# Zero stores at other spots: three behind the first group's loads, one behind the last dwd store, four ahead of the last group's first dv store

## The chip, the cores and the metric

The kernel runs on one core of one Trainium2 chip. The metric is device time of one execution in microseconds (us), lower is better.

## The reference, cut to what matters

The reference is the forward and the backward pass of one decode layer: attention of four tokens over a window of 1024 of 4096 cached keys and values, plus a gated feed-forward block, with gradients of all inputs.

```python
W = min(4096, max(256, Sk // 4))                 # 1024 of 4096
k = jnp.repeat(k_cache[:, :, Sk - W:, :], rep, axis=1)
v = jnp.repeat(v_cache[:, :, Sk - W:, :], rep, axis=1)
...
return x + _A_ref(xn, A_k_cache, A_v_cache, A_wq, A_wo) + _B_ref(xn, B_w_gate, B_w_up, B_w_down)
```

The gradients of the two caches have the caches' full shape, (4, 8, 4096, 128) in bf16. Three quarters of each are zeros, because the window does not reach them. These zeros need no arithmetic, but they are 48 MiB that must be written. They go out from one zeroed tile as 32 stores of 1.5 MB, and the kernel is free to place these stores anywhere in the order of its transfers.

## The kernel before

One queue (SyncE) issues nearly all loads and all large stores, in program order. `zero(n)` puts the next n zero stores into it:

```python
def zero(n=1):
    for _ in range(min(n, len(zlist))):
        og, b, g = zlist.popleft()
        store(nc.sync, og[b, g:g + ZR, 0:K0, :].rearrange("g (m j) d -> m g (j d)", m=P // ZR), ztile[:], "zeros")

nc.gpsimd.memset(ztile[:], 0.0)
zero(2)                                  # behind the loads of weights and of group 0
...
def piece_d(f4, i, n, held):             # one of the four stores of dwd (out_8)
    ...
    if i == 3:
        store(nc.sync, out_8[...], held["osb"]..., "rest")
        zero(f4 == 1)
...
for t in range(NT):                      # four groups
    kv_steps(t, 0, 0)
    ...
    softmax(t)
    kv_steps(t, 1, 1)
    if t == NT - 1:
        zero(3)                          # ahead of the last group's dv stores
    link(len(chain))
    ...
tick(len(bg))
zero(len(zlist))                         # what is left
```

Each dv and dk store (1 MB, staged in one of three buffers) is followed by one more zero store. The names in the profile: `ztile` is the zeroed tile, `osb_d`, `osb_g`, `osb_o`, `osb_q` are the output buffers of the weight gradients (four in rotation), `stg_dv` and `stg_dk` those of the cache gradients.

## Time and profile before

| | before |
|---|---|
| time, median of the first 3 runs | 284.95 us (284.8 to 285.53) |
| span of the profiled run | 283.4 us |
| TensorE, VectorE, ScalarE busy | 71%, 58%, 42% |
| moved by DMA | 112.12 MB, mean 396 GB/s |
| last compute instruction begins | 247.7 us |

A large transfer runs on all 16 DMA engines of the core, and the trace has one landing per engine for it. I quote the *median landing* (the ordinary engine), the *last landing* (the slowest), and the *lag*, the difference of the two. The landings carry no engine's name: "the slow engine" is the one that lands last.

### The profile page before, as it was taken

To read this page: it belongs to the slowest core of one execution; us is meant where nothing else is said; L and a number is where in the kernel's file an instruction comes from. 1 tells how busy PE (TensorE), PEld (TensorE's weight loads), DVE (VectorE), ACT (ScalarE), POOL (GpSimd) and SP (SyncE) were. 2 spreads that over 40 slices of the span, in tenths; PEclk is the share of its full clock that TensorE was granted. 3 is DMA by queue.
4 is the path that set the end of the run, shared out by engine and by line. 5 is a ranking of instruction groups with operands and counts; after the bars stand their busy time and mean duration, and the time that the engine had idled before them with its cause. 6 is when DMAs were issued, how large, how long until landed. Compare 5 with 4: busy or idle time off the path is not lost.

```text
span 283.4 us, 6866 instructions
## 1 busy us (share of the span) xinstructions
PE 200.5 (71%) x2972; PEld 137.3 (48%) x2972; DVE 163.4 (58%) x313; ACT 117.8 (42%) x219; POOL 40.1 (14%) x40
## 2 busy tenths in 40 slices
PE   0275799998798899998993799889995997300000
PEld 0264576765466754676752467665564743100000
DVE  7946646676857455767561576766776288900000
ACT  2021476662156077635371464438661387200000
POOL 8600000043011700020700002130004000000000
PEclk9999579999999999999999599999999799955555
DMA  7999989999999999999999999999999989999993
GB/s 266 391 376 433 432 334 369 370 418 351 366 428 409 419 422 422 426 427 417 410 387 423 423 426 430 410 425 404 397 415 377 415 337 420 426 418 415 422 418 153
DMA packets 19565, 112.12 MB, mean 396 GB/s; under 512 B 1664, under 2 KB 4496, under 8 KB 11088
## 3 DMA queue, kind: packets, MB, share of 16 engines
q1 hardware_dynamic: 17744, 103.56, 89.5%
q0 software_dynamic: 1632, 6.29, 5.6%
q10 hardware_dynamic: 160, 1.84, 1.8%
q8 instruction: 23, 0.38, 0.5%
q14 instruction: 6, 0.05, 0.0%
HBM read 30.68 MB, written 81.01 MB: 394 GB/s over the span
## 4 chain that ended last, share of the span: by engine, by line
PE 30%; issue 19%; DMA 18%; DVE 12%; POOL 5%; ACT 3%; DVEq 0%; POOLq 0%; ACTq 0%
DMA out_dram<-stg_dv 11%; DMA wq_sb<-in_A_wq_dram 7%; PE kv_ps L484 6%; PE T_ps L279 5%; PE od_ps L450 4%; PE S_ps L345 4%; DVE dS_s L367 2%; DVE T_sb L98 2%; PE dwq_ps L520 2%; POOL ztile L167 2%; DVE wqT L98 2%; PE pT_ps L279 2%; PE acc_ps L256 1%; PE dwo_ps L505 1%; DVE P_s L367 1%
## 5 line engine op out<-in xcount | busy, mean ns | idle before, releaser
L98 DVE COPY T_sb<-T_ps 128x1024 bf16<-128x1024 bf16 x64 | 44.1, 688 | 24.9 <-PE T_ps L279 24.7
L97 ACT CAST stg_dk<-kv_ps 128x512 bf16<-128x512 f32 x52 | 29.1, 588 | 26.3 <-PE kv_ps L484 11.5
L97 ACT CAST stg_dv<-kv_ps 128x512 bf16<-128x512 f32 x51 | 28.1, 588 | 25.1 <-PE kv_ps L484 24.4
L484 PE MATMUL kv_ps<-qmr,dS_s 128*128 128x512 bf16 x64 | 23.0, 396 | 7.3 <-ACT stg_dk L97 6.6
L463 POOL TENSOR_TENSOR o_s<-od_r,msk_r 128x512 bf16<-128x512 bf16 x8 | 9.1, 1158 | 107.9 <-DVE od_r L455 78.6
L484 PE MATMUL kv_ps<-domr,P_s 128*128 128x512 bf16 x64 | 21.1, 379 | 0.0
L279 PE MATMUL T_ps<-ident,vb 128*128 128x128 bf16 x256 | 20.3, 225 | 0.3 <-DVE T_sb L98 0.3
L279 PEld LDWEIGHTS <-vb 128*128 128x128 bf16 x256 | 17.2, 101 | 4.9 <-issue 2.7
L279 PE MATMUL T_ps<-ident,kb 128*128 128x128 bf16 x256 | 19.5, 219 | 0.0
L279 PEld LDWEIGHTS <-kb 128*128 128x128 bf16 x256 | 16.7, 98 | 4.2 <-issue 0.9
L97 ACT CAST osb_q<-dwq_ps 128x512 bf16<-128x512 f32 x25 | 14.5, 586 | 8.3 <-PE dwq_ps L520 7.4
L329 POOL TENSOR_TENSOR domr<-r,msk 128x1024 bf16<-128x1024 bf16 x4 | 7.6, 1892 | 68.4 <-DVE r L326 62.0
L97 ACT CAST osb_o<-dwo_ps 128x512 bf16<-128x512 f32 x24 | 13.8, 586 | 4.4 <-PE dwo_ps L505 3.6
L97 ACT CAST osb_g<-dwg_ps 128x512 bf16<-128x512 f32 (+1 forms) x25 | 12.5, 541 | 6.6 <-PE dwg_ps L673 5.0
L98 DVE COPY wgT<-wgT_ps 128x1024 bf16<-128x1024 bf16 x14 | 9.6, 686 | 7.7 <-PE wgT_ps L279 7.7
L345 PE MATMUL S_ps<-T_sb,qm 128*32 128x256 bf16 x128 | 12.7, 386 | 0.6 <-DVE T_sb L98 0.5
L345 PE MATMUL S_ps<-T_sb,dom 128*32 128x256 bf16 x128 | 12.7, 387 | 0.1
L98 DVE COPY woT<-woT_ps 128x1024 bf16<-128x1024 bf16 x16 | 11.0, 686 | 2.6 <-PE woT_ps L279 2.2
L98 DVE CAST stg_dk<-kv_ps 128x512 bf16<-128x512 f32 x12 | 7.9, 686 | 7.8 <-DMA out_dram<-stg_dv 7.2
L505 PE MATMUL dwo_ps<-dyr,o_s 128*128 128x512 bf16 x32 | 11.9, 388 | 0.5 <-DVE stg_dk L98 0.2
L520 PE MATMUL dwq_ps<-od_r,xnm 128*128 128x256 bf16 x64 | 11.6, 274 | 0.2 <-ACT osb_q L97 0.2
L98 DVE COPY wqT<-wqT_ps 128x1024 bf16<-128x1024 bf16 x16 | 10.5, 685 | 1.8 <-PE wqT_ps L279 1.6
(188 smaller groups left out, 377.7 us busy)
## 6 DMA issues: line engine op xcount, KB each, us to landing
out_dram<-ztile SPq DMA_DIRECT2D x32, 1536.0 KB, 19.4
kb<-in_A_k_cache_dram SPq DMA_DIRECT2D x8, 1024.0 KB, 15.7
vb<-in_A_v_cache_dram SPq DMA_DIRECT2D x8, 1024.0 KB, 20.7
out_dram<-stg_dv SPq DMA_DIRECT2D x8, 1024.0 KB, 16.7
out_dram<-stg_dk SPq DMA_DIRECT2D x8, 1024.0 KB, 16.1
out_dram<-osb_o SPq DMA_DIRECT2D x8, 512.0 KB, 19.0
out_dram<-osb_q SPq DMA_DIRECT2D x8, 512.0 KB, 11.6
out_dram<-osb_g SPq DMA_DIRECT2D x8, 448.0 KB, 7.9
```

The costliest lines, as they stand in the source:

```text
L97: return nc.scalar.copy(out=out, in_=in_)
L98: return nc.vector.tensor_copy(out=out, in_=in_)
L167: nc.gpsimd.memset(ztile[:], 0.0)
L279: nc.tensor.transpose(ps[:, i, :], a, ident[:])
L329: nc.gpsimd.tensor_tensor(out=mr[:].rearrange("p g q d -> p (g q) d"), in0=r4[:, k, :].unsqueeze(1).broadcast_to([P, SL, Dh]), in1=msk[:]. ...
L345: nc.tensor.matmul(ps[b * RB:(b + 1) * RB, :], lhsT=zt[:, b * GP + g, c0:c0 + RB], rhs=T_sb[:].rearrange("p (x b) -> p b x", b=B)[:, b, :] ...
L367: nc.vector.scalar_tensor_tensor(out=out[:], in0=src[:].unsqueeze(2).broadcast_to([P, WQ, B]), scalar=rr[:, 0:1], in1=mskb[:].unsqueeze(1) ...
L450: nc.tensor.matmul(od_ps[g * 32:g * 32 + B * rep, k, g, :], lhsT=cols[:, jj, g * NQ + q, :], rhs=blks[(t, g)][:, j, :], start=(j == 0), st ...
L463: nc.gpsimd.tensor_tensor(out=o_s[:, g], in0=rows[:, g].unsqueeze(1).broadcast_to([P, rep, Dh]), in1=msk_r[:].unsqueeze(2).broadcast_to([P ...
L484: nc.tensor.matmul(mps[:].rearrange("p q d -> p (q d)"), lhsT=src[:, j * P:(j + 1) * P], rhs=mr[:, g].rearrange("p q d -> p (q d)"), start ...
L505: nc.tensor.matmul(mps[:], lhsT=o_s[:, g].rearrange("p r d -> p (r d)")[:, i:rep * Dh:rep], rhs=dyr[:], start=True, stop=True)
L520: nc.tensor.matmul(mps[:, i].rearrange("p g d -> p (g d)"), lhsT=xnm[:, i2 * 2 + i, c * P:(c + 1) * P], rhs=dq_r[:].rearrange("p g d -> p ...
```

## The change

Its intent is to have zero stores queued where the queue waits for compute and the DMA engines run out of work. The number of zero stores stays 32; three come forward from the end.

```diff
     nc.gpsimd.memset(ztile[:], 0.0)
-    zero(2)
+    zero(3)
...
-            zero(f4 == 1)
+            zero(f4 % 2)
...
             if t == NT - 1:
-                zero(3)
+                zero(4)
```

Below, these three lines are called the front part, the dwd part and the late part.

## The prediction

> **What bounds the kernel now.** I read the page first, for the share of each engine and of the transfers, then the stretches of a microsecond each, for where the transfers pause, then the order of issue on the store queue, and last the landings of single transfers. No engine is near full on the page (TensorE 71%, VectorE 58%, ScalarE 42%). The row of the 16 DMA engines is:
>
> ```profile
> DMA  7999989999999999999999999999999989999993
> DMA packets 19565, 112.12 MB, mean 396 GB/s; under 512 B 1664, under 2 KB 4496, under 8 KB 11088
> ```
>
> Transfers are busy in nearly every slice, and compute stops near 248 us of 283 us: the chain of waits itself ends there, with the last small VectorE work, and behind it only stores run. So the bytes set the end, and time is won only where a DMA engine has nothing to do. The store queue in order of time (start us, length us, then what is issued):
>
> ```profile
> 18.55 1.69 SPq L103 DMA_DIRECT2D out_dram<-ztile  x2
> 37.73 3.53 SPq L103 DMA_DIRECT2D out_dram<-osb_d  x2
> 41.31 0.55 SPq L103 DMA_DIRECT2D out_dram<-ztile  x1
> ...
> 43.08 3.79 SPq L103 DMA_DIRECT2D out_dram<-osb_d  x2
> 49.16 0.33 SPq L103 DMA_DIRECT2D out_dram<-osb_g  x1
> ...
> 214.72 3.80 SPq L103 DMA_DIRECT2D out_dram<-ztile  x3
> 228.66 0.54 SPq L103 DMA_DIRECT2D out_dram<-stg_dv  x1
> ...
> 253.96 6.89 SPq L103 DMA_DIRECT2D out_dram<-ztile  x5
> ```
>
> The queue issues in program order and blocks on the first store whose data is not there. It stands still before 37.73, 49.16 and 228.66, and five zero stores are left for the end. In stretches of 1 us (the last two columns are the mean busy share of the 16 DMA engines and GB/s) the transfers issued before run out just there:
>
> ```profile
> 40.00:41.00 1.00, 1.00 (x19) 0.86 (x18) 0.60 (x2) 0.98 (x3) 0.00 (x0) 1.00 0.39 156
> 41.00:42.00 1.00, 1.00 (x21) 0.77 (x18) 0.60 (x2) 0.98 (x3) 0.00 (x0) 1.00 0.38 152
> 46.00:47.00 1.00, 1.00 (x20) 0.76 (x18) 0.69 (x1) 0.81 (x3) 0.00 (x0) 1.00 0.82 340
> 49.00:50.00 1.00, 0.85 (x14) 0.61 (x14) 0.69 (x2) 0.40 (x1) 0.00 (x0) 1.00 0.25 72
> 228.00:229.00 1.00, 0.97 (x13) 0.47 (x10) 0.75 (x3) 1.00 (x3) 0.00 (x0) 1.00 0.27 111
> 229.00:230.00 1.00, 0.97 (x28) 0.86 (x29) 0.69 (x2) 0.13 (x1) 0.00 (x0) 1.00 0.43 176
> 278.00:279.00 1.00, 0.00 (x0) 0.00 (x0) 0.00 (x0) 0.00 (x0) 0.00 (x0) 0.50 0.53 221
> 279.00:280.00 1.00, 0.00 (x0) 0.00 (x0) 0.00 (x0) 0.00 (x0) 0.00 (x0) 0.50 0.09 37
> 280.00:281.00 1.00, 0.00 (x0) 0.00 (x0) 0.00 (x0) 0.00 (x0) 0.00 (x0) 0.50 0.09 37
> 281.00:282.00 1.00, 0.00 (x0) 0.00 (x0) 0.00 (x0) 0.00 (x0) 0.00 (x0) 0.50 0.03 12
> ```
>
> The reader is to see two things. There are three holes, at 40 to 42, at 49 and at 228 to 230, and the change puts a zero store ahead of each. And the end is not even: from 279 us the share is 0.09, which is one or two engines of 16, for another 3 us. A single slow DMA engine ends the program.
>
> The trace has sixteen landings for each transfer, which measures that engine. I give the median landing and how far behind it the last one is. Last zero store: median 279.06, last 282.29, 3.2 us behind, second-last only 0.9 us behind. The third of the zero stores issued from 214.72: median 228.75, last 234.15, 5.4 us behind. The dv store after it: median 232.83, last 236.65. Median to median that is 4.1 us for a 1 MB store; last to last it is 2.50 us. The later 1 MB stores, with no hole in front, took 2.5 us from the last landing of the transfer ahead to their own (240.45 to 243.03, 246.74 to 249.23). So the slow engine worked straight through the hole at 228, and the other fifteen waited.
>
> **What the Trainium skill says.** "DMA: Bandwidth & Descriptors", section "Why a DMA increments its semaphore by 16 and not by 1", says that a DMA runs on up to 16 engines "that finish independently", and only the full count means landed; the spread of 0.3 to 6 us between landings agrees. The same page, "Where 436 GB/s comes from", puts the ceiling at 435 GB/s; the steady stretches here (423 to 436 GB/s, 260:270 at 436) are at it, so filling holes is the only gain from moving stores. "Issuing engines are not separate DMA queues" says that all issuers share the same 16 engines; here the weight loads that GpSimd issues took 15.4 and 21.8 us to land among the stores, which agrees.
>
> **The change part by part.** No store is added or removed: 32 zero stores of 1.5 MB each before and after. Comparing the order of instructions, nothing moves on TensorE, VectorE, ScalarE and GpSimd but buffer numbers; only the store queue differs. One zero store takes about 3.7 us of all engines (median landings of the last three: 271.64, 275.37, 279.06). The five at the end become two.
>
> Third zero store behind the loads: it is queued at about 20 to 22 us, so the engines have 3.7 us more to do when they would run dry at 40. The hole is (1-0.39)+(1-0.38) = 1.23 us on the mean engine, and it is filled. What is over (2.5 us) also carries across the dips at 46 (0.18) and 49 (0.75).
>
> The zero store behind the last dwd store: its 3.7 us lie where the first has already closed the hole. I give it nothing of its own; it makes the queue longer between 50 and 70.
>
> Fourth zero store ahead of the last dv stores: the hole at 228 to 230 is 0.73+0.57 = 1.30 us on the mean engine and is filled.
>
> Sum on the mean engine: 1.23+0.18+0.75+1.30 = 3.46 us. That would be the gain if all engines ended level.
>
> On the engine that ends last it is less. The 1.30 us at 228 count nothing, because that engine had no pause there. From about 126 us its landings follow one another without a gap that the transfers do not explain. What counts is its pause before 56 us. At 40 us the last engine is 2.2 us behind the median, more than the hole, so it lost next to nothing; the ordinary engines lost 1.2 to 1.6 us there and up to 0.9 us at 46 to 49. By 56 us the spread is down to 0.35 us: the laggards had caught up while the others waited. I cannot tell from the landings whether the engine last at the end is one of the two behind at 40 (gain about 0.4 us, for part of the second hole) or an ordinary one (about 1.2+0.9 = 2.1 us). With fourteen of sixteen ordinary, but the same engine perhaps slow throughout, I take 1.5 us. The stated prediction is 284.95-1.5 = 283.4 us.
>
> **Costs.** Stores of dwd and dwg/dwu land later: two more zero stores are 7.4 us of transfers, less about 2 us of holes, so some 5.4 us by 60 us. The output buffers come free that much later. Before, ScalarE waited 1.3 us for one of them near 64 us; after, some 3 to 5 us there, and the load of the next group's weights is issued later with it. This moves compute, not the end: queue and compute move by the same amount, and compute has room at the end, as the slow engine has 12.9 us of landings (249.84 to 262.8) between the issue and the landing of the first of the last dwq stores. The fourth zero store makes the last dv store land up to 2.4 us later (3.7 less the 1.3 of the hole), and the last dk evictions wait for its buffer; the two zero stores left at the end cover it.
>
> **Rivals.** (1) All engines gain alike, and 3.46 us go: 281.5 us. For it speaks the mean share; against it the last landings. (2) The slow engine has no pause at all and its work is fixed: no gain, 284.5 to 285 us. For it speaks the 2.2 us lag at 40; against it that the last engine may change. (3) The later buffers stall TensorE long enough that its clock falls (it reads 0.51 at 155 to 160 us after a pause) and a store comes late with the queue dry: a new hole of 1 to 3 us, 285 to 287 us. Against it: the queue is longer everywhere. (4) With the queue deeper, the small dips at 196, 205 and 216 close as well, about 1.2 us on the mean engine: 280.3 us. Against it: compute is held by landings (the dv store issued at 132.9 landed at 156.5 and held ScalarE 6.7 us), so it shifts with the queue.
>
> **Range and chances.** Between rival 1 and a little above rival 2: 281.9 to 285.1 us. Faster by over 2% needs under 279.3 us, more than all the holes named: 0.03. Slower by over 2% needs 290.7 us: 0.02. Within 2%: 0.95.
>
> **What would show it.** Shares of 0.9 and more at the first hole and at the last (which comes about 5 us later); a gap between median and last landing of the final zero store that is larger than 3.2 us, 5 us or so, with a longer tail of 0.06 to 0.09 behind the bulk; more wait of ScalarE for output buffers near 64 us; compute ending 5 to 8 us later. Wrong would be: a last gap that stays at 3 us with the end 3 us earlier (rival 1), or a share under 0.5 in a new place (rival 3).

## The result, and the profile after

| | before | after |
|---|---|---|
| time, median of 4 runs each | 285.12 us | 283.03 us (282.93 to 283.69) |
| span of the profiled run | 283.4 us | 281.0 us |
| last zero store: median landing | 279.06 us | 274.50 us |
| last zero store: last landing | 282.29 us | 279.94 us |
| lag | 3.2 us | 5.5 us |

The ratio is 0.9931 (95% interval 0.991 to 0.9951), so the change is worth about 2.0 us. Ratios here are the mean time of one kernel's fast runs over that of the other's of the same rounds, so they are not quite the ratio of the medians quoted.

The two landings tell the story in one row each. The ordinary DMA engine is done 4.56 us earlier. The slowest engine is done 2.35 us earlier, and that is what the time followed.

The landings also tell where the slowest engine won this. Each zero store put ahead of a transfer should delay it by some 3.7 us; what is missing of that delay is gain. The first dwg store (`osb_g`, two more zero stores ahead of it) landed last at 57.90 us instead of 52.36, so 7.4-5.54 = 1.9 us were won by then. The dwq store that landed last at 222.33 us before came at 227.32: 7.4-4.99 = 2.4 us (in between, the figure wavers from 1.7 to 4.4). The last dwq store, with three more ahead, came at 272.69 instead of 264.01: 11.1-8.68 = 2.4 us. So the slowest engine won nothing from the late hole. For the median landing, the same two dwq stores give 2.4 and 4.6 us.

The row of DMA slices of the kernel after, to be set against that of before. The 8s of slices 6 and 33 are gone, and the last slice is a 0, where for most of it only one engine still works:

```profile
DMA  7999999999999999999999999999999999999990
```

The store queue of the kernel after. The third zero store follows the first two, one comes at 46.42, four at 219.74, and two are left at the end:

```profile
18.53 3.75 SPq L103 DMA_DIRECT2D out_dram<-ztile  x3
38.12 2.64 SPq L103 DMA_DIRECT2D out_dram<-osb_d  x2
...
46.42 0.71 SPq L103 DMA_DIRECT2D out_dram<-ztile  x1
48.67 0.34 SPq L103 DMA_DIRECT2D out_dram<-osb_g  x1
...
219.74 4.40 SPq L103 DMA_DIRECT2D out_dram<-ztile  x4
233.63 0.54 SPq L103 DMA_DIRECT2D out_dram<-stg_dv  x1
...
263.25 1.98 SPq L103 DMA_DIRECT2D out_dram<-ztile  x2
```

The same in stretches of 1 us (the last three columns: TensorE's granted clock, mean busy share of the 16 DMA engines, GB/s):

```profile
40.00:41.00 1.00, 1.00 (x20) 0.76 (x18) 0.69 (x1) 0.98 (x3) 0.00 (x0) 1.00 1.04 434
49.00:50.00 1.00, 1.00 (x24) 0.82 (x20) 0.27 (x2) 0.89 (x2) 0.00 (x0) 1.00 0.95 393
201.00:202.00 1.00, 1.00 (x12) 0.52 (x12) 0.78 (x2) 0.75 (x2) 0.00 (x0) 1.00 0.47 193
210.00:211.00 1.00, 1.00 (x14) 0.64 (x10) 0.36 (x2) 0.86 (x4) 0.00 (x0) 1.00 0.40 160
233.00:234.00 1.00, 0.94 (x13) 0.45 (x10) 0.75 (x2) 1.00 (x3) 0.00 (x0) 1.00 0.93 393
274.00:275.00 1.00, 0.00 (x0) 0.00 (x0) 0.00 (x0) 0.00 (x0) 0.00 (x0) 0.50 0.24 98
275.00:276.00 1.00, 0.00 (x0) 0.00 (x0) 0.00 (x0) 0.00 (x0) 0.00 (x0) 0.50 0.06 25
278.00:279.00 1.00, 0.00 (x0) 0.00 (x0) 0.00 (x0) 0.00 (x0) 0.00 (x0) 0.50 0.06 25
```

The hole at 40 went from a share of 0.39 to 1.04, the one at 49 from 0.25 to 0.95. The late hole, which would now lie some 5 us later than 228, is closed (0.93). The mean engine has deeper dips than before at 201 and 210. They cost the slowest engine nothing: between 200 and 222 us (times of before) the gain of the last landing, reckoned as above, stays at 2.4 us, while that of the median falls from 4.5 to 2.4. From 275 to 279 the share is 0.06, which is one engine of sixteen at 25 GB/s, alone.

What the change cost: the gradients' output buffers come free later. Waits between 40 and 90 us for a store to land before its buffer could be written, in the kernel after (who waits, for what, us in total, times, longest):

```profile
ACT osb_g L97 <- DMA out_dram<-osb_g: 3.2, 1, 3.2
DVE osb_g L98 <- DMA out_dram<-osb_g: 2.9, 1, 2.9
ACT osb_g L97 <- DMA out_dram<-osb_d: 2.0, 1, 2.0
```

Before, there was one such wait of 1.3 us. Compute ends later (the last instruction begins at 257.21 instead of 247.74; about half of that comes from the late part, as is shown below), and the end does not care.

### The profile page after: what moved, and what is told of

Its sections match the earlier page's. It is cut to its first block, busy times and chain, and to the rows that moved or that the text cites. A ratio compares the mean times of both kernels' runs of the same rounds, so it can differ in the third digit from the quotient of the medians.

```text
span 281.0 us, 6867 instructions
## 1 busy us (share of the span) xinstructions
PE 203.1 (72%) x2972; PEld 138.8 (49%) x2972; DVE 164.1 (58%) x313; ACT 117.8 (42%) x219; POOL 40.1 (14%) x40
## 4 chain that ended last, share of the span: by engine, by line
PE 47%; DMA 22%; DVE 16%; ACT 4%; issue 2%; SPq 0%; DVEq 0%; ACTq 0%
DMA out_dram<-stg_dv 13%; PE T_ps L279 8%; PE kv_ps L484 7%; DMA wd_sb<-in_B_w_down_dram 6%; PE S_ps L345 5%; PE od_ps L450 5%; DMA out_dram<-osb_g 4%; DVE T_sb L98 3%; DVE dS_s L367 2%; PE wdT_ps L279 2%; PE dwq_ps L520 2%; PE acc_ps L256 2%; PE dwd_ps L660 2%; DVE P_s L367 2%; PE wgT_ps L279 2%
## 5 line engine op out<-in xcount | busy, mean ns | idle before, releaser
L484 PE MATMUL kv_ps<-qmr,dS_s 128*128 128x512 bf16 x64 | 23.9, 414 | 11.3 <-ACT stg_dk L97 10.6
L279 PE MATMUL T_ps<-ident,kb 128*128 128x128 bf16 x256 | 20.4, 225 | 0.0
L279 PEld LDWEIGHTS <-kb 128*128 128x128 bf16 x256 | 17.5, 101 | 4.5 <-issue 1.3
L484 PEld LDWEIGHTS <-dS_s 128*128 128x128 bf16 x64 | 6.2, 101 | 12.2 <-issue 11.1
```

The source lines that it names most:

```text
L279: nc.tensor.transpose(ps[:, i, :], a, ident[:])
L484: nc.tensor.matmul(mps[:].rearrange("p q d -> p (q d)"), lhsT=src[:, j * P:(j + 1) * P], rhs=mr[:, g].rearrange("p q d -> p (q d)"), start ...
```

## The experiments

Two theories. **A**: the one DMA engine that lands last sets the end, and a hole costs time only where that engine, too, has nothing to do. **B**: the end follows the mean engine, and each hole that is filled is worth its missing share.

### The front part alone

```diff
-    zero(2)
+    zero(3)
```

> Only the third zero store behind the first group's loads; the others stay as before. Theory A (the DMA engine that lands last sets the end, and only its pauses before 56 us count): the holes at 40 to 42 and at 49 us close, and most of the whole gain of 2.1 us comes from here, 1.5 to 2.1 us, about 283.2 us; the last landing of the last zero store comes 1.5 to 2.1 us earlier. Theory B (all engines gain what the mean engine's holes are worth): 1.23+0.18+0.75 = 2.16 us of gain here too, but with the median landing and the last one moving alike; the two theories differ in the last lag, about 4 to 5 us under A and 3.2 us under B.

Measured: 283.73 us against 285.5 us of before in the same rounds, ratio 0.9927 (0.9909 to 0.9944), 2.1 us. Last zero store: median 274.48, last 280.91, lag 6.4 us. So this line alone brings the whole gain. The median moved 4.6 us and the last landing 1.4 us in the profiled run, so they do not move alike; that is against B. The lag is above what A expected (4 to 5 us), and the 1.4 us are a little under its 1.5 to 2.1; the profiled run was the slowest of the six (283.97 us).

### The dwd part alone

```diff
-            zero(f4 == 1)
+            zero(f4 % 2)
```

> Only the zero store behind the last dwd store. It is issued near 46.4 us, after the hole at 40 to 42 us, so it can close the dip at 46 and the hole at 49 us alone. Theory A: 0.3 to 0.9 us of gain, about 284.5 us. Theory B: 0.93 us, about 284.2 us. If the first-hole pause is what the slow engine lost, this run keeps nearly all of the time of before.

Measured: 285.23 us against 285.5 us, ratio 0.9981 (0.9967 to 0.9996), 0.5 us by the ratio. Last zero store: median 278.38, last 281.92. The first hole stays open (share 0.31 at 40 us), the one at 49 is closed. Half a microsecond is in A's range; B's 0.93 us is near the edge of the interval. This run alone does not decide between them.

### The late part alone

```diff
             if t == NT - 1:
-                zero(3)
+                zero(4)
```

> Only the fourth zero store ahead of the last group's first dv store. Theory A: no gain, within 0.3 us of before (285.1 us), although the hole at 228 to 230 us closes; the median landing of the last zero store comes about 1.3 us earlier, the last landing stays, the lag grows from 3.2 to about 4.5 us. Theory B: 1.3 us of gain, 283.8 us, lag unchanged at 3.2 us.

Measured: 285.95 us against 285.5 us, ratio 1.001 (0.9997 to 1.0023). No gain. The stretches of this run at the place of the hole and at its end:

```profile
228.00:229.00 1.00, 0.94 (x13) 0.45 (x11) 0.78 (x2) 1.00 (x3) 0.00 (x0) 1.00 1.02 430
229.00:230.00 1.00, 1.00 (x28) 0.83 (x29) 0.68 (x2) 0.06 (x1) 0.00 (x0) 1.00 0.91 381
...
276.00:277.00 1.00, 0.00 (x0) 0.00 (x0) 0.00 (x0) 0.00 (x0) 0.00 (x0) 0.50 0.58 246
277.00:278.00 1.00, 0.00 (x0) 0.00 (x0) 0.00 (x0) 0.00 (x0) 0.00 (x0) 0.50 0.14 61
...
281.00:282.00 1.00, 0.00 (x0) 0.00 (x0) 0.00 (x0) 0.00 (x0) 0.00 (x0) 0.50 0.06 25
```

The hole at 228 to 230 is gone, the bulk of the stores ends two microseconds earlier (median landing 277.06 instead of 279.06), and the last landing is at 282.89 instead of 282.29. The lag is 5.8 us (A had expected 1.3 us for the bulk and a lag of 4.5). A gain of the ordinary engines, here 2.0 us, was worth nothing. This refutes B, whose 1.3 us lie far outside the interval.

### The front and the dwd part without the late part

```diff
-    zero(2)
+    zero(3)
...
-            zero(f4 == 1)
+            zero(f4 % 2)
```

> The first two parts together, without the late one. Theory A: the whole gain, 2.0 us, 283.0 us, equal to the changed kernel within 0.3 us. Theory B: 2.16 us, 1.3 us slower than the whole change is under B, so 284.3 us when scaled to the measured whole of 2.1 us.

Measured: 283.67 us against 285.5 us, ratio 0.993 (0.9911 to 0.9949), the whole gain. The late hole is open again (shares of 0.50, 0.21 and 0.55 from 232 to 235 us). Last zero store: median 276.41, last 279.82. The ordinary engines end 1.9 us later than in the kernel after, the slowest 0.1 us earlier.

### Making the late hole larger on purpose

If A holds, a much larger hole at the same place must still be free as long as the slow engine bridges it. The kernel after was taken, with two zero stores there, and then with one:

```diff
-                zero(4)
+                zero(2)        # second kernel: zero(1)
```

> The changed kernel with two zero stores instead of four ahead of the last group's first dv store; two more stand at the end. The other fifteen DMA engines then run dry about 5 us before that dv store: without the fourth store the hole was 1.3 us, and one store less adds 3.7 us. Theory A (the engine that lands last sets the end): it is about 6.0 us behind there in the changed kernel, so it still bridges the hole and the time stays within 0.5 us of the changed kernel (283 us), with the lag cut from 5.5 to 0.5 to 1.5 us at the end. Theory B (mean engine): 5 us lost, about 288 us.

> The same with one zero store there. Hole of the ordinary engines 1.3+2x3.7 = 8.7 us. Theory A: only what exceeds the lag of 6.0 us is lost, some 2 to 3.5 us, about 285.5 to 286.5 us, and the lag at the end falls under 1.5 us. Theory B: 8.7 us lost, about 291.7 us.

> The changed kernel again, for the same chip and rounds as the two above. Both theories: ratio to before near 0.993, 283 to 283.7 us.

Measured in the same rounds, before at 285.93 us:

| zero stores ahead of the last group's first dv store | time | ratio to before | last zero store: median / last landing |
|---|---|---|---|
| four (the changed kernel again) | 283.16 us | 0.9906 (0.9886 to 0.9926) | 274.76 / 279.96 |
| two | 283.90 us | 0.9931 (0.9907 to 0.9954) | 279.29 / 280.19 |
| one | 288.24 us | 1.0086 (1.0063 to 1.0108) | 284.36 / 285.22 |

With two stores, the hole of that run:

```profile
229.00:230.00 1.00, 1.00 (x15) 0.75 (x12) 0.73 (x2) 0.52 (x1) 0.00 (x0) 1.00 0.37 148
230.00:231.00 1.00, 0.99 (x12) 0.58 (x9) 1.00 (x2) 0.65 (x3) 0.00 (x0) 1.00 0.15 53
231.00:232.00 1.00, 1.00 (x15) 0.70 (x12) 0.85 (x2) 1.00 (x4) 0.00 (x0) 1.00 0.06 25
232.00:233.00 1.00, 0.94 (x13) 0.45 (x11) 0.81 (x2) 1.00 (x3) 0.00 (x0) 1.00 0.06 25
```

For two microseconds fifteen engines stand still and one works at 25 GB/s. On the mean engine 3.4 us are missing in these four lines. The ordinary engines end 4.5 us later than in the changed kernel, the time is 0.7 us worse (a little over A's 0.5, far from B's 5). The lag at the end fell to 0.9 us: the hole spent nearly all of it. The packets show that the slow engine did not pause: its last packet of the zero stores ran to 234.81 us, and its first packet of the dv store began there.

With one store, the slow engine runs dry as well:

```profile
228.00:229.00 1.00, 0.78 (x6) 0.29 (x4) 0.00 (x0) 0.59 (x2) 0.00 (x0) 0.50 0.06 25
...
231.00:232.00 1.00, 0.99 (x12) 0.57 (x10) 1.00 (x3) 0.65 (x2) 0.00 (x0) 1.00 0.00 0
...
233.00:234.00 1.00, 0.99 (x12) 0.59 (x11) 0.75 (x2) 1.00 (x3) 0.00 (x0) 1.00 0.00 0
```

Now there are microseconds with a share of 0.00, and now the hole costs 5.1 us. A expected 2 to 3.5 us and B 8.7 us, so both sizes missed. The packet records of this run show why A's did. The slow engine's last packet ended at 230.87 and the next began at 235.15, a pause of 4.3 us, where I had estimated 8.7-6.0 = 2.7 us. The lag at that place was 5.3 us and not 6.0, and the dv store was issued at 233.95, 1.4 us later than in the run with two. TensorE's granted clock was 0.50 at 228 us here; that this delayed the store is likely and not shown by itself. The remaining 0.9 us are the lag that is left at the end, but it is that of another engine. After the pause all sixteen began together (235.15 to 235.29); the one that landed the dv store 2.0 us behind the median is the one on which a 16 KB instruction fetch (queue 8, 237.63 to 238.51) stood between two packets.

### Two attempts to unload the slow engine

If one engine ends 5.5 us after the rest, sparing it bytes should beat both kernels. The Trainium skill ("DMA: Bandwidth & Descriptors", "Why a DMA increments its semaphore by 16 and not by 1") says that the number of engines is the largest count up to 16 that divides the outermost dimensions of both sides, and that the lowest-numbered ones are used. First, both last zero stores on fifteen engines:

```diff
+            if narrow:                       # the two stores left at the end
+                m0, j0 = 120 // ZR, ZW // Dh
+                store(nc.sync, og[b, g:g + ZR, 0:m0 * j0, :].rearrange("g (m j) d -> m g (j d)", m=m0),
+                      ztile[0:120, :], "zeros")
+                # (cut: the remaining 192 rows of each of the two heads, over 128 partitions)
```

> The changed kernel, with its two last zero stores issued over 120 partitions, which the Trainium skill says puts them on the 15 lowest-numbered engines of 16, and a small store over 128 partitions for the rest of each. If the engine that lands last is the sixteenth, it is spared about 3.5 us per store: its end moves from 279.9 to about 273 us, the others' from 274.8 to about 275.2 us, and the end becomes about 275.5 us of span, 4 to 4.5 us earlier (about 278.7 us of time, over 2% under the kernel before). If it is another engine, the end is the same or up to 0.5 us later. In both cases fifteen landings of each long store are late and one comes at once.

Measured: 287.6 us against 285.62 us, ratio 1.0074 (1.0055 to 1.0093), so some 4 us slower than the changed kernel (0.9931 to 1.0074 of about 285.5 us). Fifteen landings of each long store came late and one at once, as the rule says. But the slow engine took part: the last landings of the two long stores are 3.9 us apart (280.22 and 284.16), one store's worth. An engine spared the long store would have landed the small one soon after its last dwq landing (276.50), and no landing of the small one lies between 275.39 and 277.92. So it is not the sixteenth, if the rule on the lowest numbers holds, and sparing that one was useless. Worse, the packets of 12 KB slowed down, from a 95th percentile of 0.47 us in the changed kernel's last part to 1.14 us. The skill's page "SBUF — State Buffer", "Door 1: The DMA port swizzle", says that a DMA reaches the partitions through 16 ports, each of two groups of four partitions; if 120 partitions are cut into fifteen runs of eight, which is assumed here, two engines may read through one port at a time. No run here shows the ports or the cut, so this cause is only argued.

Second, the very last zero store on eight engines:

```diff
+                for gi in range(ZR):
+                    store(nc.sync, og[b, g + gi, 0:K0, :].rearrange("(m e j) d -> e m (j d)", e=8, m=P // 8),
+                          ztile[:, 0:ZW // ZR], "zeros")
```

> The changed kernel with its very last zero store issued as two stores of half the size with an outermost dimension of 8, which by the Trainium skill's rule on the count of engines puts them on eight engines, the lowest-numbered, each with twice the bytes. This locates the slow engine, it is no test of A against B. If it is one of the other eight, it is spared 3.7 us and ends near 276.2 us of span while the eight end near 278.2: about 1.7 us earlier than the changed kernel, 281.4 us. If it is one of the eight, it ends 3.7 us later, about 286.7 us. Eight late landings for each of these two stores are expected.

Measured: 288.83 us against 285.93 us, ratio 1.0102 (1.0075 to 1.0129). Eight late landings per store, as expected. The last landings are 278.47 for the ordinary zero store ahead of them and 282.17 and 285.87 for the two half stores: the slow engine was among the eight and paid 3.7 us for each half store. The time is still 2.1 us above the 286.7 us expected for this case: already the ordinary zero store took the slow engine 5.8 us (272.63 to 278.47) instead of 3.6, which stays unexplained. By the rule, the slow engine is one of the eight lowest-numbered. No version that beats the changed kernel came of this; with the layouts tried, a store that leaves out one engine in the middle is not to be had.

## Why the prediction was right

The prediction was 283.4 us, range 281.9 to 285.1 and 0.95 for "within 2%". Measured were 283.03 us. The mechanism held; that the number came within 0.4 us is in part luck, since the 1.5 us were a weighing between two cases (0.4 and 2.1 us) that the landings could not tell apart. Point by point:

- *A single slow DMA engine ends the program.* Shown. In the kernel after, the second-last landing (275.50) is 4.4 us ahead of the last. With the late part alone the median landing fell by 2.0 us and the time did not change; with the late hole enlarged the median rose by 4.5 us and the time changed by 0.7 us.
- *The 1.30 us at 228 count nothing.* Shown by the late part alone (1.001) and by leaving it out (0.993 without, 0.9931 and 0.9906 with it).
- *The pause before 56 us counts; 0.4 us or 2.1 us, taken as 1.5.* The term was somewhat too small: the front part alone gave 2.1 us. That is the figure for "an ordinary engine at 40 us". It fits that the engine that ends last was not one of the two behind at 40 us, but the landings carry no engine's name, so the identity is argued, not shown. That the gain was won before the late hole is shown by the landings above: 1.9 of the 2.4 us of the last landing stood at the first dwg store, all of them by 222 us.
- *3.46 us on the mean engine, were all engines level.* Too small: the median landing gained 4.56 us, the mean of the sixteen landings 4.35 (279.31 to 274.96). Where the rest came from was not looked for.
- *Nothing of its own for the dwd part.* Beside the front part it added nothing (0.993 against 0.9927). Alone it gave 0.5 us, for the hole at 49.
- *The lag at the end grows to 5 us or so.* 5.5 us.
- *ScalarE waits 3 to 5 us for output buffers.* 3.2+2.0 us. VectorE waited 2.9 us as well, which I had not named.
- *Compute ends 5 to 8 us later.* It was 9.5 us. Without the late part it was 4.9 (the last instruction begins at 252.64 us), near the 5.4 us that the prediction had for the first two parts. The other 4.6 us come with the late part, 3.7 of them as a longer wait: ScalarE waits 4.6 us instead of 0.9 for the first of the last group's two dv stores to land, before it can fill that buffer with dk. The prediction named this wait and gave the dv store up to 2.4 us of delay, a zero store less the hole. But the slow engine has no hole there: that store's last landing went from 236.65 to 245.32 us, and of these 8.67 us 4.97 are its later issue and 3.7 the whole zero store.
- *Rival 3.* The granted clock of TensorE did fall around the stall (0.63 and 0.69 from 60 to 70 us, where it was 1.00 before); how much of the 4.9 us that is was not tested. The new hole on the slow engine did not come.
- *The small dips near 200 and 210 stay.* They grew on the mean engine (0.47 and 0.40). The slow engine was 5 to 7 us behind there and worked through them; that they grew because loads and buffers wait for the slowest engine is argued, not shown.

What stays open is why that engine is slow. It needs about 3.9 to 4.3 us for a zero store between 175 and 225 us and 3.65 us after compute has ended, where the ordinary engines need 3.7 us. Where it worked alone, with the other fifteen standing still (one zero store ahead of the dv store), its 12 KB packets still took 464 to 568 ns instead of 460. So its slowness is not a queue for shared bandwidth with the others. Nor is it the instruction fetches: in the run with two stores the fetch at 236.26 to 237.15 us lies on another engine, while the slow one moves dv packets. What else slows it while the compute engines are busy, the records do not say.

## What to carry to other kernels

When a kernel is bound by its transfers, as this one is, look at the last of the sixteen landings and not at the mean share of the DMA engines: a hole is worth only what it takes from the engine that ends last. A hole shorter than that engine's lag was nearly free here (0.7 us for 3.4), and filling it moves only the engines that wait at the end anyway; the holes early on, before a lag had built up, were the ones to fill. A quick test is to enlarge the suspected hole on purpose and see whether the time moves.

## What the Trainium skill lacked or had wrong

- "DMA: Bandwidth & Descriptors" does not say that the lag of one engine of sixteen can carry over from transfer to transfer until it sets the end of a whole program. Here it ended 3.2 us after the median before the change and 5.5 us after, and a hole that cost the mean engine 3.4 us cost 0.7 us of time.
- The same page, "Latency and other measured facts", says that engines 7 and 15 are usually slower and guesses at the descriptor rings of GpSimd's DMAs. Here the slow engine took part in a store on the fifteen lowest-numbered engines, so by the page's own rule on numbers it is not the last one (engine 7 stays possible), and its lag grew from 3.2 us (median landings at 168 us) to 5.3 us (at 192 us) of the kernel before, with none of GpSimd's transfers between.
- The same page's rule for the count of engines held (fifteen and eight late landings), but no page warns that a store on fifteen engines over 120 partitions can be slower: 95th percentile of a 12 KB packet 1.14 us instead of 0.47 us, with the median packet nearly unchanged (0.48 instead of 0.46 us).
